# Running both halves' w2 sums ahead of their wo sums, a new share of MLP pieces among the attention units, and final wo sums that end one at a time

## The chip, the cores and the metric

One Trainium2 chip, one core. The metric is device time in microseconds (us) of one execution; lower is better. Executions of one kernel differ by 1 to 3 us, so a difference of a few us is read from two sources here: the clock, over several rounds on the same chip, and the trace, in which the start of every instruction is recorded.

## The reference, cut to what matters

The output is `x + A(xn) + B(xn)` with `xn = layernorm(x)`, 2048 tokens, width 1024. A is attention in four segments of 512 tokens with 32 heads of 32, plus a memory carried from segment to segment, and an output projection `wo`. B is a token-mixing MLP, `w2(gelu(w1 h))` along the token axis with a hidden size of 3584.

```python
for s in range(4):                                   # segment
    logits = einsum('bhqd,bhkd->bhqk', qs, ks) * scale + mask
    a_dot  = einsum('bhqk,bhkd->bhqd', softmax(logits), vs)
    num, den = phi(qs) @ M, phi(qs) @ z + 1e-06      # memory of the segments before
    o = g * num / den + (1 - g) * a_dot
    M, z = M + phi(ks)^T vs, z + sum(phi(ks))
A = concat(o) @ wo
B = (gelu(h^T w1 + b1) @ w2 + b2)^T                  # h = layernorm(xn)
```

## The kernel before: the parts that matter

The program first runs layernorm and the hidden layer of the MLP (896 matmuls of 128x512), which needs no attention. Then come 32 attention units, eight per segment, each with four heads. Each unit has three exponentiations on ScalarE (ACT), of about 1.9, 1.5 and 1.5 us in the trace. So that TensorE (PE) need not wait for them, pieces of the second MLP layer and of the output projection are put in between. One piece is one 128x512 matmul. Matmuls write into PSUM banks, eight buffers numbered 0 to 7 in this program; a bank can be written anew only when another engine has read its last result. There are 16 output chunks of 128 tokens and each has two halves of 512 columns. A half is a sum of 28 w2 pieces; for the twelve chunks of segments 0 to 2 ("fused" chunks), 8 wo pieces are added in the same PSUM bank. The chunks of segment 3 (12 to 15) come first, without wo; their wo sums are made in a tail.

In the code below, `logits` multiplies q by k, `weigh` multiplies the exponentials by v, and `combine` divides and gates on VectorE. The output of `combine` is transposed into one block of `oT` per unit, which the wo pieces read. The "k phi" is phi(k), made on ScalarE and VectorE after each k projection.

```python
def main_emit(self, n):                    # emit the next n pieces
    ...
    j, c, half, fused = self.main[self.main_k]     # one half after the other: 28 w2, then 8 wo
    b = self.main_bank                             # banks 6 and 7 in turn
    ...                                            # matmuls
    if end == total:
        fw.op("dve", lambda e: e.scalar_tensor_tensor(dst, self.bank(b), self.b2c[:, c:c + 1], dst, ...))  # bias add
        ...
        self.main_bank = 13 - b

def attention_and_out(self):
    ...
    for c in range(4):
        self.proj_v(0, c, c)
    for u in range(self.LEAD):             # LEAD = 2
        self.proj_q(u, 4 + u); self.proj_k(u, 6 + u)
        ...
    for u in range(N_UNIT):
        n0, n1, n2 = (9, 7, 6) if s == 0 else (10, 8, 8)      # n3: 6 or 10; 28 or 36 in all
        self.logits(u, 0)                  # 32-row matmuls into banks 0-3, then exp on ACT
        if u: self.combine(u - 1)          # VectorE
        self.main_emit(n0)
        self.logits(u, 1); self.main_emit(n1)
        self.logits(u, 2)
        ...                                # DMA transposes of k and of the combined output
        self.main_emit(n2)
        self.weigh(u, 0); self.weigh(u, 1)
        if un < N_UNIT: self.proj_q(un, 0)           # un = u + 2, bank 0
        self.weigh(u, 2)
        if m < 2 * N_SEG: self.proj_v(m, u % 4, 2)
        self.weigh(u, 3)
        if un < N_UNIT: self.proj_k(un, 1)           # bank 1
        self.main_emit(n3)
    self.main_emit(10 ** 6)
    self.tail()

def tail(self):
    self.combine(u)                        # unit 31
    ...                                    # load chunks 12-15 back: fin[0..3]
    for (i, h), b in zip(order, banks):    # eight sums of seven products ...
        if b == 3: self.o_transpose(u, 3)  # PE transpose and ACT copy ahead of the last
        ...
    for (i, h), b in zip(order, banks):    # ... then the eighth product of each
        ...
        fw.op("dve", ... tensor_tensor(dst, self.bank(b), dst, op=ALU.add))
        if h == 1: fw.dma(self.out_d[:, 4 * s + i, :], fin[i][:], ...)
```

The softmax here doesn't subtract the row's maximum and nothing guards it: scores larger than these inputs give would overflow.

## Time and profile before

| | before |
|---|---|
| time, median of the runs beside the changed kernel | 721.57 us (720.23 to 722.08) |
| span of the profiled execution | 720.2 us |
| PE busy | 97% |
| VectorE (DVE), ACT busy | 37%, 38% |
| from the last hidden-layer matmul to the end | 509.20 us |

Three lines of the page: its heading, the busy time of each engine with its share of the span and the number of instructions, and the shares of the chain of waits that ended last.

```profile
span 720.2 us, 11218 instructions
PE 701.0 (97%) x4818; PEld 324.6 (45%) x4818; DVE 263.1 (37%) x577; ACT 276.7 (38%) x314; POOL 111.1 (15%) x151
...
PE 93%; DVE 3%; ACT 2%; DMA 1%; issue 1%; SPq 0%; POOL 0%; DVEq 0%; ACTq 0%
```

PE bounds the kernel. How full it is can't be read from the 97%: a 128x512 matmul is recorded as 379 ns, but in the trace two of them start 215.5 ns apart, so the recorded end lies some 160 ns after the next one's start and hides short gaps. The Trainium skill says the same of this busy time (Perfetto Trace Analysis, "Identifying the Most-Contended Engine": it is not a good measure of how close a kernel is to its limit, because matmuls are pipelined), and its TensorE: Matmul & The Clock Gate, "Wait — 56ns, not 53.3ns?", gives 215.7 ns from start to start at 512 columns. So in what follows a wait is the time from one start to the next, less 0.2155 us per 512 columns, and less the 0.10 us that a change into or out of the 32-row logits costs in every unit.

Who waited for whom on PE (engine, line, what released it, us in total, times, longest; L192 is the helper that issues every matmul, so it tells the tile and not the place):

```profile
PE ps_all L192 <- POOL h L651: 3.5, 2, 2.7
PE ps_all L192 <- DVE h L647: 3.5, 1, 3.5
PE ps_all L192 <- ACT etmp_1584 L749: 2.2, 8, 0.3
PE ps_all L192 <- DVE warm L508: 1.3, 1, 1.3
PE ps_all L192 <- ACT pT L786: 1.0, 1, 1.0
PE ps_all L192 <- ACT xnT_69 L884: 0.7, 1, 0.7
PE ps_all L198 <- DMA brow_51<-in_B_b_dram: 0.4, 1, 0.4
PE ps_all L192 <- DVE ost_1579 L826: 0.4, 1, 0.4
PE ps_all L192 <- DVE ost_1580 L826: 0.4, 1, 0.4
```

Lines 1, 2, 4 and 7 belong to the start of the program, which the change does not touch. The others are the waits in the attention part and the tail that this list shows: eight of 0.3 us, one of 1.0, three of 0.4 to 0.7. Here is one of the eight, from the timeline around the start of unit 2 (start us, duration us, engine, line, operation, out<-in; in brackets the idle time before it and what ended it):

```profile
252.74 1.46 PE L192 MATMUL ps_all<-gT,w2h_912 128*128 128x512 bf16 x6
252.94 0.69 DVE L746 CAST kT_1570<-ps_all 128x512 bf16<-128x512 f32 x1 [0.90 <-PE ps_all L192]
253.73 0.60 ACT L749 ACTIVATE etmp_1584<-ps_all 128x512 bf16<-128x512 f32 x1 [2.55 <-DVE kT_1570 L746]
...
254.47 0.40 PE L192 MATMUL ps_all<-qT_1569,kT_1572 32*128 32x512 bf16 x4 [0.27 <-ACT etmp_1584 L749]
```

The k projection ends at 252.74 in bank 1. The bank is free when a cast (0.69) and an exponentiation (0.60) have read it, and only then may the next unit's logits write it, 1.73 us later. Six pieces take 6 x 0.2155 = 1.29 us. With the switch of 0.10, 0.33 us are lost. And the tail (the end of the ACT copy; the last two adds and stores):

```profile
709.82 0.39 PE L198 MATMUL ps_all<-ident,o_s_1582 128*128 128x128 bf16 x4
710.25 0.60 ACT L884 ACTIVATE xnT_69<-ps_all 128x512 bf16<-128x512 bf16 x1 [15.09 <-PE ps_all L198]
...
710.90 0.39 PE L192 MATMUL ps_all<-wo_sb,xnT_69 128*128 128x512 bf16 x1 [0.69 <-ACT xnT_69 L884]
...
716.44 1.27 DVE L1016 TENSOR_TENSOR fin_7771<-ps_all,fin_7771 128x512 bf16<-128x512 f32 x2
716.54 0.33 SPq L214 DMA_DIRECT2D out_dram<-fin_7770  x1
717.74 0.33 SPq L214 DMA_DIRECT2D out_dram<-fin_7771  x1
```

The last matmul starts at 713.93. All eight sums end within 1.5 us, so their eight adds queue on VectorE until 717.71, and the last store follows: 6.3 us from the last matmul's start to the end of the span.

### The profile page before, as it was taken

What the parts mean: (1) busy time and instruction counts of PE and PEld (TensorE: products, weight loads), DVE (VectorE), ACT (ScalarE), POOL (GpSimd) and SP (SyncE); (2) the same over time, 40 slices, a digit from 0 to 9 for tenths busy, and PEclk for the clock granted to TensorE, in tenths of its full rate; (3) what the DMA queues carried; (4) which work ended last, traced back from release to release, by engine and by line L of the source; (5) the groups of instructions that cost most, each with busy time, mean ns of one, the idle gap of its engine ahead of it and who ended that gap; (6) DMA issues with size and microseconds to landing.
All of it is one profiled execution on the core that took longest, in us unless ns stands there. A gap on an engine that the chain in (4) does not pass through costs nothing.

```text
span 720.2 us, 11218 instructions
## 1 busy us (share of the span) xinstructions
PE 701.0 (97%) x4818; PEld 324.6 (45%) x4818; DVE 263.1 (37%) x577; ACT 276.7 (38%) x314; POOL 111.1 (15%) x151
## 2 busy tenths in 40 slices
PE   6899999999999999999999999999999999999996
PEld 2344444444444444444444444444444444444442
DVE  4970000000002343344444545544555544344452
ACT  4551122111225445445444444443444444434420
POOL 1540000000001112211221111222111122111220
PEclk9999999999999999999999999999999999999999
DMA  9549677246016373872654625355352635527103
GB/s 269 142 115 177 144 190 192 64 112 124 12 60 163 66 125 87 127 118 63 123 117 87 126 44 126 75 109 120 79 125 45 126 86 97 111 53 117 30 27 114
DMA packets 211515, 77.17 MB, mean 107 GB/s; under 512 B 172554, under 2 KB 203274, under 8 KB 211466
## 3 DMA queue, kind: packets, MB, share of 16 engines
q1 hardware_dynamic: 211248, 76.43, 48.9%
q8 instruction: 38, 0.62, 0.4%
q14 instruction: 11, 0.09, 0.0%
q10 hardware_dynamic: 218, 0.02, 0.0%
HBM read 59.79 MB, written 5.24 MB: 90 GB/s over the span
## 4 chain that ended last, share of the span: by engine, by line
PE 93%; DVE 3%; ACT 2%; DMA 1%; issue 1%; SPq 0%; POOL 0%; DVEq 0%; ACTq 0%
PE ps_all L192 93%; DMA xin<-in_A_x_dram 1%; ACT etmp_1584 L749 1%; DVE kT_1570 L746 0%; DVE ln_st L606 0%; DVE kT_1572 L746 0%; DVE kT_1571 L746 0%; DVE ln_st L605 0%; ACT pT L786 0%; SPq L214 0%; DVE h L647 0%; ACT L749 0%; POOL h L651 0%; DVE fin_7771 L1016 0%; DVE fin_7770 L1016 0%
## 5 line engine op out<-in xcount | busy, mean ns | idle before, releaser
L786 ACT ACTIVATE pT<-ps_all 128x1536 bf16<-128x1536 f32 (+1 forms) x96 | 153.0, 1593 | 96.8 <-PE ps_all L192 96.8
L792 POOL TENSOR_SCALAR_AFFINE_SELECT pT<-pT 128x512 bf16<-128x512 bf16 x128 | 90.9, 723 | 561.5 <-ACT pT L786 561.5
L708 ACT ACTIVATE gT<-ps_all,b1c 128x512 bf16<-128x512 f32 x56 | 37.7, 689 | 134.5 <-PE ps_all L192 134.5
L192 PE MATMUL ps_all<-h,w1s_78 128*128 128x512 bf16 x320 | 73.9, 385 | 7.1 <-POOL h L651 3.5
L192 PE MATMUL ps_all<-h,w1s_79 128*128 128x512 bf16 x320 | 73.8, 385 | 0.0
L746 DVE CAST kT_1570<-ps_all 128x512 bf16<-128x512 f32 x11 | 7.6, 690 | 178.9 <-PE ps_all L192 178.9
L192 PE MATMUL ps_all<-gT,w2h_912 128*128 128x512 bf16 x224 | 56.3, 380 | 0.0
L192 PE MATMUL ps_all<-gT,w2h_914 128*128 128x512 bf16 x224 | 56.3, 380 | 0.0
L192 PE MATMUL ps_all<-h,w1s_80 128*128 128x512 bf16 x256 | 55.9, 379 | 0.0
L192 PE MATMUL ps_all<-gT,w2h_913 128*128 128x512 bf16 x224 | 53.9, 381 | 0.0
L192 PE MATMUL ps_all<-gT,w2h_911 128*128 128x512 bf16 x224 | 53.9, 381 | 0.0
L192 PEld LDWEIGHTS ps_all<-h,w1s_78 128*128 128x128 bf16 x320 | 31.4, 99 | 46.3 <-issue 8.5
L192 PEld LDWEIGHTS ps_all<-h,w1s_79 128*128 128x128 bf16 x320 | 31.7, 99 | 39.0 <-issue 2.3
L826 DVE CAST ost_1579<-ps_all 128x264 bf16<-128x264 f32 (+1 forms) x64 | 23.8, 394 | 69.2 <-PE ps_all L192 69.0
L826 DVE CAST ost_1580<-ps_all 128x264 bf16<-128x264 f32 (+1 forms) x64 | 23.8, 394 | 69.0 <-PE ps_all L192 68.9
L192 PEld LDWEIGHTS ps_all<-h,w1s_80 128*128 128x128 bf16 x256 | 25.0, 98 | 30.2
L749 ACT ACTIVATE etmp_1584<-ps_all 128x512 bf16<-128x512 f32 x24 | 14.3, 597 | 58.1 <-DVE kT_1572 L746 20.7
L192 PEld LDWEIGHTS ps_all<-gT,w2h_912 128*128 128x128 bf16 x224 | 20.6, 98 | 25.2 <-issue 2.5
L192 PEld LDWEIGHTS ps_all<-gT,w2h_914 128*128 128x128 bf16 x224 | 20.5, 98 | 24.7 <-issue 2.5
L192 PEld LDWEIGHTS ps_all<-gT,w2h_911 128*128 128x128 bf16 x224 | 19.3, 98 | 25.3 <-issue 6.4
L192 PEld LDWEIGHTS ps_all<-gT,w2h_913 128*128 128x128 bf16 x224 | 19.3, 98 | 25.3 <-issue 6.4
L192 PE MATMUL ps_all<-wo_sb,oT_1587 128*128 128x512 bf16 x128 | 30.2, 379 | 0.0
(154 smaller groups left out, 815.3 us busy)
## 6 DMA issues: line engine op xcount, KB each, us to landing
w1s_80<-in_B_w_dram SPq DMA_DIRECT2D x4, 1024.0 KB, 5.9
w1s_78<-in_B_w_dram SPq DMA_DIRECT2D x4, 1024.0 KB, 5.6
w1s_79<-in_B_w_dram SPq DMA_DIRECT2D x4, 1024.0 KB, 5.7
wq_907<-in_A_wq_dram SPq DMA_DIRECT2D x16, 256.0 KB, 3.5
wq_908<-in_A_wq_dram SPq DMA_DIRECT2D x16, 256.0 KB, 3.6
wk_909<-in_A_wk_dram SPq DMA_DIRECT2D x16, 256.0 KB, 3.8
wk_910<-in_A_wk_dram SPq DMA_DIRECT2D x16, 256.0 KB, 4.0
w2h_911<-in_B_w_dram SPq DMA_DIRECT2D x8, 448.0 KB, 4.8
```

The costliest lines, as they stand in the source:

```text
L192: ins = self.nc.tensor.matmul(*args, **kwargs)
L708: fw.op("act", lambda e: e.activation(self.gT[:, fc, half * 512:(half + 1) * 512], self.bank(b), ACT.Gelu_apprx_tanh, bias=self.b1c[:, fc: ...
L746: fw.op("dve", lambda e: e.tensor_copy(self.kT[k][:], self.bank(b)), reads=[self.R_bank[b]], writes=[self.R_kT[k]])
L749: fw.op("act", lambda e: e.activation(self.etmp[1][:], self.bank(b), ACT.Exp), reads=[self.R_bank[b]], writes=[self.R_etmp[1]])
L786: fw.op("act", lambda e: e.activation(self.pT[:, :, off:off + total], self.ps[:, 0:4, 0:total], ACT.Exp, scale=SCALE), reads=self.R_bank[0:4],
L792: fw.op("pool", lambda e: e.affine_select(d, d, pattern=[[0, 4], [1, P]], compare_op=ALU.is_ge, fill=0.0, base=0, channel_multiplier=-1), ...
L826: fw.op("dve", lambda e: e.tensor_copy(dst, self.ps[:, b, 0:n * VW]), reads=[self.R_bank[b]], writes=[self.R_ost[o][qb]])
```

## The change

Its intent: keep PE from waiting, with the same 4818 matmuls. (1) Within a fused chunk the w2 sums of both halves come first (bank 6 and bank 7), then the two wo sums. The first wo piece of a chunk is then 56 pieces after its start, not 28, so a chunk may begin earlier, before its segment's attention is finished. (2) That allows more pieces in the first segment: 32 per unit, 8 before unit 0, 34 per unit later, and pieces in place of the q projection that units 30 and 31 lack. (3) At the start q0 and k0 are projected ahead of v. (4) The final sums end one at a time and each half row is stored by itself. (5) `combine` is moved: behind the first pieces of the next unit, and for the last unit of a segment to that unit's own end, so that its block is there sooner.

```diff
     def main_init(self):
-        for n, c in enumerate(self.mlp_order):
-            for half in range(2):
-                self.main.append((n, c, half, c < 12))
+        for j, c in enumerate(self.mlp_order):
+            self.main += [(j, c, half, a, a + 14) for half in range(2) for a in (0, 14)]
+            if c < 12:
+                self.main += [(j, c, half, N_FCH, N_FCH + N_GRP) for half in range(2)]
 ...
-            b = self.main_bank
+            b, s = 6 + half, c // 4
 ...
     def attention_and_out(self):
+        self.proj_q(0, 4)
+        self.proj_k(0, 5)
+        self.k_transpose(0)
         for c in range(4):
             self.proj_v(0, c, c)
-        for u in range(self.LEAD):
-            self.proj_q(u, 4 + u)
-            self.proj_k(u, 6 + u)
-            if u == 0:
-                self.k_transpose(0)
+        self.proj_q(1, 4)
+        self.proj_k(1, 5)
+        self.main_emit(8)
 ...
             self.logits(u, 0)
-            if u:
-                self.combine(u - 1)
+            if u and last_of_seg(u - 1):
+                self.o_transpose_dma(u - 1)
             self.main_emit(n0)
+            if u and not last_of_seg(u - 1):
+                self.combine(u - 1)
 ...
             if un < N_UNIT:
                 self.proj_q(un, 0)
+            else:
+                self.main_emit(8)
 ...
+            if last_of_seg(u):
+                self.combine(u)
             self.main_emit(n3)
 ...
+    def share(u):
+        if u < N_UNIT - 4:
+            return (10, 8, 7, 7) if u < N_GRP else (10, 8, 8, 8)
+        return (10, 9, 8, 10) if u < N_UNIT - 2 else (10, 9, 8, 4)
 
     def tail(self):
-        order = [(i, h) for i in range(4) for h in range(2)]       # and two loops over all eight sums
 ...
+        def product(n, j0, j1):                                    # matmuls j0..j1-1 of sum n
 ...
+            fw.dma(self.out_d[:, 4 * s + i, h * 512:(h + 1) * 512], dst, reads=[R_fin[i][h]],
+                   writes=[self.R_out[4 * s + i]], is_output=True)
+
+        product(0, 0, 7)
+        product(1, 0, 7)
+        self.o_transpose(u, 6)
+        product(2, 0, 7)
+        for n in range(3):
+            product(n, 7, 8)
+        for n in range(3, 8):
+            product(n, 0, 8)
```

More of the change, by code (lines that the diff above doesn't have):

```diff
@@ L889, in main_init @@
         self.main = []
-        for n, c in enumerate(self.mlp_order):
-            for half in range(2):
-                self.main.append((n, c, half, c < 12))
+        for j, c in enumerate(self.mlp_order):
+            self.main += [(j, c, half, a, a + 14) for half in range(2) for a in (0, 14)]
+            if c < 12:
+                self.main += [(j, c, half, N_FCH, N_FCH + N_GRP) for half in range(2)]
         self.main_k = 0
         self.main_at = 0
-        self.main_bank = 6
     def main_emit(self, n):
@@ L899, in main_emit @@
         while n > 0 and self.main_k < len(self.main):
-            j, c, half, fused = self.main[self.main_k]
-            b = self.main_bank
-            at = self.main_at
-            total = N_FCH + (N_GRP if fused else 0)
-            if at == 0 and half == 0:
-                self.stg_ring.ensure(j)
-            s = c // 4
-            if at < N_FCH:
-                w, R_w = self.w2_ring.get(2 * j + at // 14)
-                end = min(at + n, (at // 14 + 1) * 14)
-                reads = [R_w] + [self.R_gT[fc][half] for fc in range(at, end)]
-            else:
-                end = min(at + n, total)
-                reads = [self.R_wo] + [self.R_oT[s % 2][jc - N_FCH] for jc in range(at, end)]
+            j, c, half, a, stop = self.main[self.main_k]
@@ new lines, in main_emit @@
+            a += self.main_at
+            end = min(a + n, stop)
+            total = N_FCH + (N_GRP if c < 12 else 0)
+            b, s = 6 + half, c // 4
+            if a == 0 and half == 0:
+                self.stg_ring.ensure(j)
+            if a < N_FCH:
+                w, R_w = self.w2_ring.get(2 * j + a // 14)
+                reads = [R_w] + [self.R_gT[fc][half] for fc in range(a, end)]
+            else:
+                reads = [self.R_wo] + [self.R_oT[s % 2][x - N_FCH] for x in range(a, end)]
@@ L914, in main_emit @@
             with fw.group(reads=reads, writes=[self.R_bank[b]]):
-                for x in range(at, end):
-                    st, sp = x == 0, x == total - 1
+                for x in range(a, end):
                     if x < N_FCH:
-                        fw.mm(self.bank(b), w[:, x % 14, :], self.gT[:, x, half * 512:(half + 1) * 512],
-                              start=st, stop=sp)
-                    else:
-                        jc = x - N_FCH
-                        fw.mm(self.bank(b), self.oT[s % 2][:, jc, (c % 4) * P:(c % 4 + 1) * P],
-                              self.wo_sb[:, jc, half * 512:(half + 1) * 512], start=st, stop=sp)
@@ L924, in main_emit @@
-            n -= end - at
-            self.main_at = end
+                        lhs, rhs = w[:, x % 14, :], self.gT[:, x, half * 512:(half + 1) * 512]
+                    else:
+                        lhs = self.oT[s % 2][:, x - N_FCH, (c % 4) * P:(c % 4 + 1) * P]
+                        rhs = self.wo_sb[:, x - N_FCH, half * 512:(half + 1) * 512]
+                    fw.mm(self.bank(b), lhs, rhs, start=(x == 0), stop=(x == total - 1))
+            n -= end - a
+            self.main_at += end - a
@@ L926, in main_emit @@
+            if end == stop:
+                self.main_k += 1
+                self.main_at = 0
             if end == total:
-                k = j % 3
-                dst = self.stg[k][:, half * 512:(half + 1) * 512]
+                stg, R_stg = self.stg[j % 3], self.R_stg[j % 3]
+                dst = stg[:, half * 512:(half + 1) * 512]
                 fw.op("dve", lambda e: e.scalar_tensor_tensor(dst, self.bank(b), self.b2c[:, c:c + 1], dst,
                                                               op0=ALU.add, op1=ALU.add),
-                      reads=[self.R_bank[b], self.R_b2c, self.R_stg[k]], writes=[self.R_stg[k]])
+                      reads=[self.R_bank[b], self.R_b2c, R_stg], writes=[R_stg])
@@ L932, in main_emit @@
                 if half == 1:
-                    fw.dma(self.out_d[:, c, :], self.stg[k][:], reads=[self.R_stg[k]], writes=[self.R_out[c]],
-                           is_output=True)
-                self.main_bank = 13 - b
-                self.main_at = 0
-                self.main_k += 1
+                    fw.dma(self.out_d[:, c, :], stg[:], reads=[R_stg], writes=[self.R_out[c]], is_output=True)
     def attention_and_out(self):
@@ L944, in attention_and_out, with last_of_seg @@
         self.stg_ring.ensure(0)
+        self.proj_q(0, 4)
+        self.proj_k(0, 5)
+        self.k_transpose(0)
         for c in range(4):
             self.proj_v(0, c, c)
-        for u in range(self.LEAD):
-            self.proj_q(u, 4 + u)
-            self.proj_k(u, 6 + u)
-            if u == 0:
-                self.k_transpose(0)
+        self.proj_q(1, 4)
+        self.proj_k(1, 5)
+        self.main_emit(8)
+        def last_of_seg(u):
+            return u % N_GRP == N_GRP - 1
         for u in range(N_UNIT):
             s = u // N_GRP
-            n = 28 if s == 0 else 36
-            n0, n1, n2 = (9, 7, 6) if s == 0 else (10, 8, 8)
-            n3 = n - n0 - n1 - n2
-            if u == 2 * N_GRP - N_GRP + 0:
+            un, m = u + self.LEAD, u // 4 + 1
+            n0, n1, n2, n3 = self.share(u)
+            if u == N_GRP:
                 wait = _after(*[self.R_xnT[c] for c in range(4)])
@@ L962, in attention_and_out @@
             self.logits(u, 0)
-            if u:
+            if u and last_of_seg(u - 1):
+                self.o_transpose_dma(u - 1)
+            self.main_emit(n0)
+            if u and not last_of_seg(u - 1):
                 self.combine(u - 1)
-            self.main_emit(n0)
             self.logits(u, 1)
@@ L970, in attention_and_out @@
                 self.k_transpose(u + 1)
-            if u:
+            if u and not last_of_seg(u - 1):
                 self.o_transpose_dma(u - 1)
@@ L975, in attention_and_out @@
             self.weigh(u, 1)
-            un = u + self.LEAD
             if un < N_UNIT:
                 self.proj_q(un, 0)
+            else:
+                self.main_emit(8)
             self.weigh(u, 2)
-            m = u // 4 + 1
             if m < 2 * N_SEG:
@@ L985, in attention_and_out @@
                 self.proj_k(un, 1)
+            if last_of_seg(u):
+                self.combine(u)
             self.main_emit(n3)
-        self.main_emit(10 ** 6)
+        assert self.main_k == len(self.main)
         self.tail()
+    @staticmethod
+    def share(u):
+        if u < N_UNIT - 4:
+            return (10, 8, 7, 7) if u < N_GRP else (10, 8, 8, 8)
+        return (10, 9, 8, 10) if u < N_UNIT - 2 else (10, 9, 8, 4)
     def tail(self):
         fw = self.fw
-        s = N_SEG - 1
+        s, u = N_SEG - 1, N_UNIT - 1
         e = _Arena(self.nc, self.early_base, self.early_end)
@@ L996, in tail @@
         R_fin = [[Res(f"fin{i}_{h}", wait) for h in range(2)] for i in range(4)]
-        u = N_UNIT - 1
-        self.combine(u)
         for i in range(4):
@@ L1001, in tail @@
                    record_reads=False)
-        order = [(i, h) for i in range(4) for h in range(2)]
-        banks = [6, 7, 0, 1, 2, 4, 5, 3]
-        for (i, h), b in zip(order, banks):
-            if b == 3:
-                self.o_transpose(u, 3)
-            with fw.group(reads=[self.R_wo] + self.R_oT[s % 2][0:7], writes=[self.R_bank[b]]):
-                for jc in range(7):
-                    fw.mm(self.bank(b), self.oT[s % 2][:, jc, i * P:(i + 1) * P],
-                          self.wo_sb[:, jc, h * 512:(h + 1) * 512], start=(jc == 0), stop=False)
-        for (i, h), b in zip(order, banks):
-            with fw.group(reads=[self.R_wo, self.R_oT[s % 2][7]], writes=[self.R_bank[b]]):
-                fw.mm(self.bank(b), self.oT[s % 2][:, 7, i * P:(i + 1) * P],
-                      self.wo_sb[:, 7, h * 512:(h + 1) * 512], start=False, stop=True)
+        def product(n, j0, j1):
+            i, h, b = n // 2, n % 2, (0, 1, 2, 3, 4, 5, 7, 6)[n]
+            with fw.group(reads=[self.R_wo] + self.R_oT[s % 2][j0:j1], writes=[self.R_bank[b]]):
+                for jc in range(j0, j1):
+                    fw.mm(self.bank(b), self.oT[s % 2][:, jc, i * P:(i + 1) * P],
+                          self.wo_sb[:, jc, h * 512:(h + 1) * 512], start=(jc == 0), stop=(jc == N_GRP - 1))
+            if j1 < N_GRP:
+                return
             dst = fin[i][:, h * 512:(h + 1) * 512]
@@ L1017, in tail @@
                   reads=[self.R_bank[b], R_fin[i][h]], writes=[R_fin[i][h]])
-            if h == 1:
-                fw.dma(self.out_d[:, 4 * s + i, :], fin[i][:], reads=R_fin[i], writes=[self.R_out[4 * s + i]],
-                       is_output=True)
+            fw.dma(self.out_d[:, 4 * s + i, h * 512:(h + 1) * 512], dst, reads=[R_fin[i][h]],
[8 more added lines that the diff above has]
+            product(n, 0, 8)
 _INS = ['A_x', 'A_wq', 'A_wk', 'A_wv', 'A_wo', 'A_beta', 'B_x', 'B_w1', 'B_b1', 'B_w2', 'B_b2']
```

## The prediction

> **What bounds the kernel now.** TensorE: the chain of waits puts 93% of the 720.2 us on PE matmuls, 3% on VectorE. Busy time overstates it: a 128x512 matmul is recorded as 379 ns, while two follow each other every 0.2155 us (timeline, start to start). The Trainium skill has the same (TensorE: Matmul & The Clock Gate, "Wait — 56ns, not 53.3ns?": 215.7 ns), so I count starts. After 30 us nearly every matmul starts when its predecessor has streamed. About 0.11 us is lost at each change into the 32-row logits; the skill's TensorEngine Tiling (Array Packing), "Key Properties", says that changing tiling mode drains the array. That stays.
>
> Waits left over, from start times:
> - unit 0: the second logits wait 1.1 us for the first exponentiation, delayed by copies and an activation of 1.28 us that come together;
> - the next eight units' first logits wait 0.32 us beyond the switch (chain: PE, cast 0.70, exp 0.61, PE): six pieces (1.29 us) don't cover the 1.73 us from the end of the k projection until bank 1 is free;
> - units 30 and 31, which have no projections: 0.46 us each, a weigh waiting for its bank's cast;
> - tail: 0.69 us for the ScalarE copy of the transposed block, then 6.3 us from the last matmul's start, since all eight sums end together: eight VectorE adds at 0.61 us, then a store that takes 2.5 us from the last add to the span's end.
>
> **What the change does.** Matmuls, bytes and ScalarE work stay; only waits can go.
> - Start: q0/k0 first, eight MLP pieces before unit 0: -1.1.
> - Seven pieces at the end of a first-segment unit: 1.51 us of cover; 8 x 0.215 = -1.7.
> - Pieces in place of the missing q projection: -0.9.
> - Transpose: the copy is covered by the third product (-0.7), but the last combine (2.5 us after the casts, a bias add before it) has just two products (3.0 us) ahead of the transpose: +0.5. Net -0.2.
> - One add (0.68 us) and a half-size store after the last matmul: 6.3 becomes 3.5: -2.8.
> - New: a fused chunk's bank 6 is needed again 8 pieces after its wo sum ends. At the end of a unit the bias add (0.75) stands behind the k phi (ends 2.64 us after the last k projection matmul), done at 3.36. By the piece order only chunk 1 to 2 (unit 10 to 11) needs the bank earlier, at 2.6: +0.8. Unit 8 first reads the last oT block 6.7 us after unit 7's k projection; combine, issue and DMA transpose (2.4 to 3.5 us from issue) need 6.3 to 7.4: +0.2.
>
> Sum: -5.7 us.
>
> **Prediction.** 715.6 us, eight times in ten between 713.0 and 718.2. Faster by over 2%: 0.02; within 2%: 0.97; slower by over 2%: 0.01.
>
> **What would show it.** Unit period in segment 0 about 14.76 us (14.11, plus four pieces, less 0.21); segments 1 and 2 about 15.19 (15.62 less two pieces); no 1.1 us gap in unit 0; 3.5 us from the last matmul's start to the end; one gap of 0.5 to 0.9 us early in unit 11, before chunk 2's first piece.
>
> **What would make it wrong.** More bank stalls than one, because bias adds queue behind combine on VectorE; oT transposes landing late behind weight loads; a late last combine; half-row stores that land no sooner than full ones.

## The result, and the profile after

The changed kernel took 714.76 us (median of four runs, 714.27 to 715.41) against 721.57 us before: 6.8 us less. The ratio is 0.9909, with a 95% interval of 0.9892 to 0.9926. A ratio here is the mean time of one kernel's fast runs over that of the other's of the same rounds, so it is not quite the ratio of the medians. That is within 2%, and the interval is well clear of 1.

```profile
span 712.6 us, 11149 instructions
PE 693.8 (97%) x4728; PEld 323.6 (45%) x4818; DVE 263.0 (37%) x577; ACT 276.9 (39%) x314; POOL 105.4 (15%) x151
...
PE 94%; DVE 2%; issue 1%; DMA 1%; ACT 0%; SPq 0%; POOL 0%; ACTq 0%
```

PE shows 4728 matmuls in place of 4818, but the weight loads are still 4818: no work has gone, 90 records are missing from this trace, one in about fifty. Each hole looks like a gap of exactly one piece. Such holes make up most of the line "issue" below; they are not waits.

```profile
PE ps_all L192 <- DVE h L647: 4.4, 1, 4.4
PE ps_all L192 <- POOL h L651: 2.6, 2, 2.2
PE ps_all L192 <- issue: 2.0, 12, 0.2
PE ps_all L192 <- DVE warm L508: 1.3, 1, 1.3
PE ps_all L192 <- DVE stg_1591 L930: 0.7, 1, 0.7
PE ps_all L198 <- DVE o_s_1582 L868: 0.3, 1, 0.3
```

All the waits of the attention part of before are gone from this list, and two are new: one for a bias add (`stg`) and one for the last combine (`o_s`). The start of unit 2 now:

```profile
254.07 1.24 PE L192 MATMUL ps_all<-gT,w2h_913 128*128 128x512 bf16 x5
254.27 0.69 DVE L746 CAST kT_1570<-ps_all 128x512 bf16<-128x512 f32 x1 [0.90 <-PE ps_all L192]
...
255.05 0.60 ACT L749 ACTIVATE etmp_1584<-ps_all 128x512 bf16<-128x512 f32 x1 [2.55 <-DVE kT_1570 L746]
255.15 0.59 PE L192 MATMUL ps_all<-gT,w2h_914 128*128 128x512 bf16 x2
...
255.79 0.40 PE L192 MATMUL ps_all<-qT_1569,kT_1572 32*128 32x512 bf16 x4
```

From the end of the k projection (254.07) to the logits (255.79) it is still 1.72 us, but seven pieces now lie in between. About 0.12 us of the 0.33 is left, too short to show in the list. The new wait in unit 11, before chunk 2's first piece:

```profile
389.36 0.69 DVE L719 SCALAR_TENSOR_TENSOR mtmp_1586<-kT_1570,mtmp_1586 128x512 bf16<-128x512 bf16 x1
...
389.56 0.60 PE L192 MATMUL ps_all<-wo_sb,oT_1587 128*128 128x512 bf16 x2
...
389.97 1.61 DVE L930 SCALAR_TENSOR_TENSOR stg_1591<-ps_all,b2c,stg_1591 128x512 bf16<-128x512 f32 x2
...
390.86 0.38 PE L192 MATMUL ps_all<-gT,w2h_911 128*128 128x512 bf16 x1 [0.69 <-DVE stg_1591 L930]
```

Two bias adds stand together in the third line. The first must empty bank 6 before chunk 2 can begin in it, and it starts only when VectorE is done with the k phi (first line). The tail:

```profile
698.39 0.40 PE L198 MATMUL ps_all<-ident,o_s_1582 128*128 128x128 bf16 x4 [0.25 <-DVE o_s_1582 L868]
...
709.62 0.69 DVE L1021 TENSOR_TENSOR fin_7792<-ps_all,fin_7792 128x512 bf16<-128x512 f32 x1 [1.03 <-PE ps_all L192]
710.37 0.33 SPq L214 DMA_DIRECT2D out_dram<-fin_7792  x1
```

One add and one half-row store follow the last matmul (its start is 709.20): 3.36 us to the end of the span in place of 6.30.

**A steadier measure.** The part before attention differs from execution to execution. In the thirteen profiles in the fast state the last hidden-layer matmul starts between 208.89 and 211.97 us, a range of 3.1 us in work that no kernel here changes. After that point two executions of the same kernel agree to 0.01 us (501.92 and 501.91 us to the end, for the changed kernel; it is the only pair of traces of one kernel in the fast state). So besides the time by the clock each experiment gets "the rest": the span less the start of the last hidden matmul. Before: 720.23 - 211.03 = 509.20. After: 712.56 - 210.64 = 501.92. The change is worth 7.28 us; the 7.7 us between the two spans holds 0.4 us of luck. Figures of the rest below are good to about 0.01 us.

### The profile page after: what moved, and what is told of

It reads as the page before. It is cut to its first block, busy times and chain, and to the rows that moved or that the text cites. A ratio compares the mean times of both kernels' runs of the same rounds, so it can differ in the third digit from the quotient of the medians.

```text
span 712.6 us, 11149 instructions
## 1 busy us (share of the span) xinstructions
PE 693.8 (97%) x4728; PEld 323.6 (45%) x4818; DVE 263.0 (37%) x577; ACT 276.9 (39%) x314; POOL 105.4 (15%) x151
## 4 chain that ended last, share of the span: by engine, by line
PE 94%; DVE 2%; issue 1%; DMA 1%; ACT 0%; SPq 0%; POOL 0%; ACTq 0%
PE ps_all L192 94%; DMA xin<-in_A_x_dram 1%; DVE ln_st L606 0%; DVE ln_st L605 0%; SPq L214 0%; DVE h L647 0%; DVE prod L864 0%; POOL h L651 0%; ACT junk L615 0%; ACT ln_rs L635 0%; DVE stg_1591 L930 0%; DVE stg_1589 L930 0%; DVE kT_1570 L746 0%; DVE ln_rs L634 0%; DVE fin_7792 L1021 0%
## 5 line engine op out<-in xcount | busy, mean ns | idle before, releaser
L792 POOL TENSOR_SCALAR_AFFINE_SELECT pT<-pT 128x512 bf16<-128x512 bf16 x128 | 84.9, 676 | 565.0 <-ACT pT L786 565.0
L192 PE MATMUL ps_all<-gT,w2h_913 128*128 128x512 bf16 x219 | 55.2, 380 | 0.4 <-issue 0.2
L192 PE MATMUL ps_all<-gT,w2h_911 128*128 128x512 bf16 x220 | 53.9, 380 | 1.0 <-DVE stg_1591 L930 0.7
L192 PE MATMUL ps_all<-gT,w2h_912 128*128 128x512 bf16 x215 | 53.6, 380 | 1.0 <-issue 0.8
L192 PE MATMUL ps_all<-gT,w2h_914 128*128 128x512 bf16 x217 | 53.9, 380 | 0.6 <-issue 0.3
```

What stands on the lines that cost most here:

```text
L192: ins = self.nc.tensor.matmul(*args, **kwargs)
L792: fw.op("pool", lambda e: e.affine_select(d, d, pattern=[[0, 4], [1, P]], compare_op=ALU.is_ge, fill=0.0, base=0, channel_multiplier=-1), ...
```

## The experiments

The theory from the prediction: PE's work is fixed, the time is that work plus a few waits, and they add up. Rivals: the gain comes from one part (the reorder itself, or the tail, or the mere number of pieces per unit), and waits that go are partly given back elsewhere. "Before" was timed beside each. All results were correct.

| run | median us | ratio to before (95%) | the rest, us |
|---|---|---|---|
| before | 720.32 to 721.57 | 1 | 509.20 |
| the change | 714.76 | 0.9909 (0.9892 to 0.9926) | 501.92 |
| r_after (the change again) | 713.07 | 0.9894 (0.9878 to 0.9909) | 501.91 |
| tail_only | 718.59 | 0.9959 (0.9946 to 0.9972) | 505.85 |
| reorder_only | 726.96 | 1.0078 (1.0066 to 1.0091) | 515.14 |
| first_only | 712.63 | 0.9879 (0.9865 to 0.9892) | 501.05 |
| seg0_front | 715.70 | 0.9931 (0.9918 to 0.9945) | 504.46 |
| old_start_8 | 713.28 | 0.9903 (0.9887 to 0.9920) | 501.90 |
| new_start_0 | 713.80 | 0.9910 (0.9895 to 0.9924) | 502.61 |
| no_qslot | 716.60 | 0.9937 (0.9921 to 0.9954) | 503.56 |
| no_qslot_own | 715.01 (the five fast runs alone 714.28) | 0.9905 (0.9888 to 0.9923) | not used |
| no_qslot_own_again | 714.08 | 0.9900 (0.9883 to 0.9918) | 502.49 |
| three_first | 712.86 | 0.9882 (0.9864 to 0.9901) | 500.60 |
| all_four | 712.86 | 0.9882 (0.9866 to 0.9898) | 499.66 |

The "slow state" is that of one execution, whose trace shows a granted TensorE clock of 0.655 where all the others have 0.99. Several expectations missed by the clock: r_after, first_only, seg0_front and old_start_8 came 1 to 2 us below their marks, which were reckoned from the change's first 714.76 us, and no_qslot and all_four came about 1 us above theirs. In the rest most came within 0.1 us of what was expected; reorder_only lost 0.3 us more, and no_qslot 0.7.

### r_after: the change once more

> The change itself again, for its spread beside the three others. Expected 714.8 us (713.8 to 715.8), and in its trace the same single stall of 0.85 us in unit 11 and unit periods of 14.65 and 15.19 us, to 0.02 us. If the stall was an accident of one execution, it is absent or elsewhere.

Measured: 713.07 us, below the expected range. The wait in unit 11 is 0.852 us (0.854 the first time), the unit periods are 14.65 and 15.19 us. The stall comes back in the same place, so it was not an accident of one execution.

### tail_only: the kernel before with the new tail alone

```diff
-        for (i, h), b in zip(order, banks):   # both loops
+        product(0, 0, 7)                      # as in the change, after self.combine(u)
+        ...
```

> The kernel before with only the new tail. Theory (the waits add up, and the tail is worth about half of the whole): 3.2 us from the last matmul's start to the end in place of 6.3, the wait around the transpose 0.4 in place of 0.7, so 3.3 us faster than before, about 718.2 us; unit periods as before (14.11, 15.62). Rival (the gain lies in the new share of the pieces, and the tail's adds were hidden behind the stores): under 1 us faster, 720.5 or more.

Measured: 718.59 us, the rest 3.35 us shorter than before. The last matmul's start to the end took 3.35 us, and the wait at the transpose 0.43 in place of 0.85 from start to start: 2.94 + 0.42 = 3.36. The unit periods are those of before. The theory holds, and the tail is a little under half of the change's 7.28 us.

### reorder_only: the kernel before with the new order of sums alone

```diff
-                self.main.append((n, c, half, c < 12))
+            self.main += [(j, c, half, a, a + 14) for half in range(2) for a in (0, 14)]
+            if c < 12:
+                self.main += [(j, c, half, N_FCH, N_FCH + N_GRP) for half in range(2)]
```

> The kernel before with only the new order of sums (both halves' w2 sums first, banks 6 and 7 fixed), its old share. Theory (the order only makes the new share possible and by itself costs bank waits): a chunk then takes exactly two units and ends at the end of one, so the next chunk's first piece waits for the bias add standing behind the k phi: about 0.8 us at the start of units 10, 12, 14, 16, 18, 20 and 22 (seven waits; none after that, as the last segment has no k phi), 5.6 us slower than before, about 727 us. Rival (the reorder itself is a gain, keeping wo sums away from late oT blocks): same or faster than before, 721.5 or less.

Measured: 726.96 us, 0.8% slower than before, the rest 5.93 us longer. The first line of the list of PE's waits and one of the seven places:

```profile
PE ps_all L192 <- DVE stg L930: 5.6, 7, 0.8
```

```profile
370.60 1.61 DVE L930 SCALAR_TENSOR_TENSOR stg<-ps_all,b2c,stg 128x512 bf16<-128x512 f32 x2
...
371.49 0.38 PE L192 MATMUL ps_all<-gT,w2h 128*128 128x512 bf16 x1 [0.80 <-DVE stg L930]
```

Seven waits at the starts of units 10, 12, 14, 16, 18, 20 and 22, as expected. From start to start each is 0.86 us, and the two-unit period grows by 0.85: 7 x 0.85 = 5.95. The reorder by itself is a loss. It pays only together with a share of pieces that puts nearly all chunk ends elsewhere, which the changed kernel's 34 pieces per unit do, with one exception.

### first_only: both halves ahead only where it is needed

```diff
-            self.main += [(j, c, half, a, a + 14) for half in range(2) for a in (0, 14)]
-            if c < 12:
-                self.main += [(j, c, half, N_FCH, N_FCH + N_GRP) for half in range(2)]
+            w2 = [[(j, c, half, a, a + 14) for a in (0, 14)] for half in range(2)]
+            wo = [[(j, c, half, N_FCH, N_FCH + N_GRP)] if c < 12 else [] for half in range(2)]
+            self.main += w2[0] + w2[1] + wo[0] + wo[1] if c % 4 == 0 else w2[0] + wo[0] + w2[1] + wo[1]
```

> The change, but both halves' w2 sums run ahead only in the first chunk of each segment (0, 4, 8); the other chunks as before, one half after the other, so that a bank comes back after 36 pieces, not 8. Theory (the wait in unit 11 is the bank, given back late): the 0.85 us gap is gone and nothing else moves, 0.85 us faster than the change, about 714.0. Rival (the gap is the weights of chunk 2 or the x tile arriving late): the gap stays in unit 11 and the time is that of the change.

Measured: 712.63 us, the rest 501.05, so 0.87 us less than the change. No wait for a bias add is left on PE, and unit 11's period is 15.19 us like its neighbours'. The wait was the bank. Only the first chunk of a segment meets blocks that are not there yet; the others gain nothing from having both halves ahead.

### seg0_front: the same number of pieces, in other places

```diff
-            return (10, 8, 7, 7) if u < N_GRP else (10, 8, 8, 8)
+            return (12, 8, 6, 6) if u < N_GRP else (10, 8, 8, 8)
```

> The change with the same 32 pieces in each first-segment unit, but placed 12, 8, 6, 6 in place of 10, 8, 7, 7. Theory (what counts is that seven pieces lie between the k projection and the next unit, and seven between the last logits and the q projection): the waits of before come back, 0.22 us more before each of units 1 to 8 and about 0.10 more before each q projection, period 14.97 in place of 14.65, 8 x 0.32 = 2.5 us slower than the change, about 717.3. Rival (it is the number of pieces in a unit that covers ScalarE): period stays 14.65, time that of the change.

Measured: 715.70 us, the rest 2.54 us longer than the change's; period 14.97 us. Before the logits 0.33 us are lost again and before the q projection 0.10. The number of pieces in a unit does not cover ScalarE; the number between one use of a bank and the next does. The 0.10 us is a wait that the prediction had overlooked: the q projection writes bank 0, which the unit's last exponentiation (1.45 us) still reads when only six pieces lie between them.

### old_start_8 and new_start_0: the order or the eight pieces

```diff
 # old_start_8
-        self.proj_q(0, 4); self.proj_k(0, 5); self.k_transpose(0)
         for c in range(4):
             self.proj_v(0, c, c)
-        self.proj_q(1, 4); self.proj_k(1, 5)
+        self.proj_q(0, 4); self.proj_k(0, 6); self.k_transpose(0)
+        self.proj_q(1, 5); self.proj_k(1, 7)
         self.main_emit(8)
 # new_start_0: the change without
-        self.main_emit(8)
```

> The change with the old order at the start (v, then q0, k0, q1, k1 in banks 4, 6, 5, 7) but with its eight pieces before unit 0. If the eight pieces are what removed the 1.1 us wait of unit 0: no such wait, time that of the change within 0.3 us. If it was the order (q0 and k0 ahead of v): the 1.1 us wait is back, about 715.9.

> The change with its new order at the start but without the eight pieces before unit 0 (they are done at the end, where the share has eight to spare). If the eight pieces are what counts: unit 0's second logits wait 0.7 to 1.0 us again. If the order is: no wait there. All later pieces come eight earlier in the order, so other bank waits may appear and are read from the trace; the verdict is the gap in unit 0, not the time.

Measured: with the old order and eight pieces there is no wait in unit 0 and the rest is 501.90 us, that of the change. With the new order and no pieces unit 0 waits 0.71 us. So the eight pieces remove the wait; beside them the order adds nothing, and without them it helps only in part (0.71 in place of 1.10; of these 0.39 us, 0.22 are the time of one piece, since ten pieces in place of nine lie ahead of the second logits). The total of new_start_0 is 0.70 us longer than the change's although two other waits went (0.85 and 0.41); the next run shows why.

### no_qslot, no_qslot_own and its repetition: pieces for the missing q projection

```diff
 # no_qslot
             if un < N_UNIT:
                 self.proj_q(un, 0)
-            else:
-                self.main_emit(8)
 ...
-        return (10, 9, 8, 10) if u < N_UNIT - 2 else (10, 9, 8, 4)
+        return (10, 9, 8, 10) if u < N_UNIT - 2 else (10, 9, 8, 12)
```

> The change without the pieces in place of the missing q projection in units 30 and 31; they are done at the end of the unit. Theory: the wait of the third weigh for its bank's cast is back, 0.46 us in each of the two units, so 0.9 us slower than the change, about 715.7; the last combine then has pieces ahead of it and the transpose may wait less, up to 0.4 us of that given back. Rival (the slot is worth nothing): time that of the change.

Measured: 716.60 us, the rest 1.65 us longer than the change's. The two waits are back, 0.52 us each from start to start, and the transpose waits no more (0.41 less): 0.63 us. Another 1.05 us was not foreseen. The last store came late; the last add and the stores around it:

```profile
711.14 0.69 DVE L1019 TENSOR_TENSOR fin<-ps_all,fin 128x512 bf16<-128x512 f32 x1 [1.03 <-PE ps_all L192]
...
712.93 0.33 SPq L214 DMA_DIRECT2D out_dram<-fin  x1
```

The add ends at 711.83, the store is issued at 712.93. The records of landings show the store before it landing at 712.87. In the change's tail both half-row stores of a block claim the same output resource, so the second waits until the first has landed. All stores leave one queue in order, so the next pair waits behind them. That makes four pairs in a row, 2.2 to 2.7 us each, and the chain begins when the first add is done. With the first adds late, the last store is late. To test it, the claim was taken away; the two halves write different columns, and each store still waits for its own add.

```diff
 # no_qslot_own, and no_qslot_own_again
-            fw.dma(self.out_d[:, 4 * s + i, h * 512:(h + 1) * 512], dst, reads=[R_fin[i][h]],
-                   writes=[self.R_out[4 * s + i]], is_output=True)
+            fw.dma(self.out_d[:, 4 * s + i, h * 512:(h + 1) * 512], dst, reads=[R_fin[i][h]], is_output=True)
```

> The kernel without pieces in the q slot (it took 503.57 us from the last hidden matmul to the end, 1.67 more than the change, where 0.92 was expected), with one line undone: the two half-row stores of a block no longer both claim the same output resource. Theory (the second half's store waits until the first half's has landed, 1.8 to 2.2 us after its issue, so the four pairs form a chain that was late at the end): the last store is issued right after the last add, 1.05 us sooner, 502.5 us from the last hidden matmul to the end. Rival (half-row stores are simply slow to issue or to land when several are under way): 503.5 again, the last store issued a microsecond after the last add.

The profiled execution was slow (1019 us, granted clock 0.655), so its trace was not used.

> The kernel of no_qslot_own once more, unchanged, because its profile fell in the slow state (granted clock 0.655), where the matmuls between two stores take half as long again and hide the question. In the fast state: theory (the second half-row store waited for the first to land) 502.5 us from the last hidden matmul to the end, the last store issued within 0.05 us of the last add; rival (half-row stores are slow by themselves) 503.5, the last store a microsecond after the last add.

```profile
710.21 0.69 DVE L1019 TENSOR_TENSOR fin<-ps_all,fin 128x512 bf16<-128x512 f32 x1 [1.03 <-PE ps_all L192]
710.93 0.33 SPq L214 DMA_DIRECT2D out_dram<-fin  x1
```

Measured: the rest 502.49 us, 1.08 less than no_qslot. The add ends at 710.90 and the store is issued at 710.93. The rival falls. In the changed kernel the same chain is there and just not late: its last store was issued at 710.37, the store before it landed at 710.31 and the last add ended at 710.31. (The pairs before it did not hold it up: the first store of the last pair was issued at 708.61, just after its own add.) And in new_start_0 the span ends 4.62 us after the last matmul's start, in place of 3.36: the same cause, by the same signs (a last store at 710.01, after an add that ended at 708.69 and a store that landed at 709.95), though there it was not tested by itself.

### three_first and all_four: taking the rest away

```diff
 # three_first = first_only, and
-        product(0, 0, 7); product(1, 0, 7)
+        for n in range(3):
+            product(n, 0, 7)
         self.o_transpose(u, 6)
-        product(2, 0, 7)
-        for n in range(3):
+        product(3, 0, 7)
+        for n in range(4):
             product(n, 7, 8)
-        for n in range(3, 8):
+        for n in range(4, 8):
             product(n, 0, 8)
 # and the stores of no_qslot_own.   all_four = three_first, and
-            return (10, 8, 7, 7) if u < N_GRP else (10, 8, 8, 8)
+            return (10, 7, 7, 8) if u < N_GRP else (10, 8, 8, 8)
```

> The kernel with both halves ahead in chunks 0, 4 and 8 only, and three products (not two) before the transpose, a fourth to cover its ScalarE copy, and the stores of the halves free of each other. Expected: no wait before the transpose (0.41 us gone), no wait after it, last store right after the last add: 500.6 us from the last hidden matmul to the end, against 501.05 without this and 501.9 in the change. If the first adds, which come later, hold back the rest: 501.0 or more.

> The same with the first segment's 32 pieces placed 10, 7, 7, 8: the eighth at the end of the unit covers the 0.12 us left before each of units 1 to 8, and seven after the second logits were enough in the kernel before. Expected: unit period 14.53 in place of 14.65, 0.94 us less, 499.7 us from the last hidden matmul to the end; about 711.0 to 711.8 us by the clock, 1.3% faster than before. If seven pieces in the middle don't cover the exponentiation of the second logits: the wait moves there and the period stays at 14.65.

Measured: the rest is 500.60 us for three_first and 499.66 us for all_four, whose first-segment period is 14.53 us. Apart from the holes of missing records, no wait longer than 0.06 us is left on PE from unit 0 to the last matmul. What PE's list of waits shows for all_four:

```profile
PE ps_all L192 <- DVE h L647: 3.9, 1, 3.9
PE ps_all L192 <- POOL h L651: 3.6, 2, 2.7
PE ps_all L198 <- DMA brow<-in_B_b_dram: 2.0, 1, 2.0
PE ps_all L192 <- issue: 1.7, 11, 0.2
PE ps_all L192 <- DVE warm L508: 1.3, 1, 1.3
```

Only the start of the program and the holes. By the trace all_four is 2.25 us shorter than the change in the part after the hidden layer. By the clock it is 1.2% faster than before (0.9882); it took 712.86 us, where 711.0 to 711.8 were expected. Against the change (0.9909 and 0.9894) the intervals overlap, and it does not differ from three_first at all (712.86 both). The profiled executions show how that can be: in all_four's the last hidden matmul started at 211.97 us, in three_first's at 210.16.

## Why the prediction was right, point by point

The predicted time was 715.6 us (713.0 to 718.2), the measured one 714.76 (713.07 in r_after). The terms, against the waits from start to start in the two traces:

| term | predicted us | measured us | shown by |
|---|---|---|---|
| wait in unit 0 | -1.1 | -1.10 | trace; the eight pieces, old_start_8 and new_start_0 |
| first logits of units 1 to 8 | -1.7 | 8 x (0.333 - 0.117) = -1.73 | trace, seg0_front |
| q projection in units 0 to 7 | not seen | 8 x 0.103 = -0.82 | trace, seg0_front |
| units 30 and 31 | -0.9 | 2 x 0.52 = -1.04 | trace, no_qslot |
| transpose in the tail | -0.2 | 0.414 - 0.853 = -0.44 | trace, tail_only |
| after the last matmul | -2.8 | 3.36 - 6.30 = -2.94 | trace, tail_only |
| bank 6, chunk 1 to 2 | +0.8 | +0.85 | trace, first_only |
| last oT block in unit 8 | +0.2 | 0 | trace |
| sum | -5.7 | -7.22 (rest: -7.28) | |

**What held.** The main claim: matmuls stay, only waits can go, and they add up on PE. The place of the one new stall was found from the order of the pieces alone, and the run that should have had seven of them had seven, in the units named. The segment 1 and 2 period came out at 15.19 us as stated.

**What was off.** By the trace the sum was 1.6 us too small (5.7 for 7.28). The first difference by the clock, 6.8 us, hides part of that; the one of r_after, 8.1 us, does not. The largest slip is a term that was missing: the first-segment period was put at 14.76 us and came out at 14.65. The shortest wait on the prediction's list has 0.32 us; the wait of 0.10 us before each q projection is not on it and occurs eight times. Together these are worth about as much as the one bank stall. Second, the wait at the transpose was counted as 0.69 us, the idle time after the recorded end; from start to start it was 0.85. The same correction makes 0.46 us into 0.52 for units 30 and 31. Third, the last oT block: the DMA transpose landed by 348.19 us and PE reached it at 348.65, so its 0.2 us never came; it took 2.48 us from issue, near the lower end of the 2.4 to 3.5 us that were reckoned with. Fourth, "q0/k0 first" was listed with the eight pieces as the cure for unit 0; the order is worth nothing beside the pieces.

**What was right by luck.** The tail's term counted an add and a store. It did not see that the half-row stores wait for one another. In this kernel the first store of the last pair lands 1.70 us after its issue, and the adds come 1.73 us apart, so the last store is free just when the last add is done; in no_qslot the chain cost 1.05 us.

The start of the program is outside the argument: the two spans differ by 7.67 us, of which 0.39 come from an earlier end of the hidden layer in the second one.

## What to carry to other kernels

When one engine is full, a change that moves work around can win only the waits, so list every wait from start to start, short ones too, and multiply by how often each occurs: 0.10 us eight times weighs as much as one stall of 0.85. Filler works by its place, between a bank's last reader and its next writer, not by its amount; and an order of sums that gives a bank back late must be checked against where in the other engine's queue the read-out falls. When one store is split into two, check that the two don't claim the same resource in the program, or the second waits for the first to land, as here.

## What the Trainium skill lacked or had wrong

- TensorE: Matmul & The Clock Gate, "Back-to-back issue gap", gives about 131 ns per matmul as the sustained rate of weight load and matmul pairs at 512 columns and about 81 ns at 128. In every trace here in the fast state such pairs start 215.5 ns apart at 512 columns (over two thousand pairs in each, every matmul with its own weight load), and the four transposes of 128 columns in the tail of before 56 ns apart. The section's other formula, which it gives for an isolated matmul (512 columns over 2.4 GHz plus 2.5 ns), fits.
- TensorEngine Tiling (Array Packing), "Key Properties", says that changing the tiling mode drains the array, but not what that costs. Here a matmul of 32 rows starts 0.10 us later than a 128-row one would after the same predecessor (0.312 us from start to start in place of 0.2155), in every unit, whatever fills it. That the drain is what takes this time is not shown.
- DMA: Bandwidth & Descriptors, "Anatomy of one DMA", gives a fixed cost of about 2.0 us for a DMA, with a fit made on the GpSimd path, and no such fit for the sync engine's queue. In the changed kernel a half-row store of 128 KB from the sync engine's queue had landed 1.70 us after its issue (708.61 to 710.31); the four full-row stores of 256 KB in the tail of before took 2.0 us.
- Perfetto Trace Analysis does not say that matmul records can be missing: 4728 of 4818 in the changed kernel's trace, one in about fifty, each hole looking like a gap of one matmul. The count of weight loads (4818) shows it.
- No page consulted has the slow state of a program on one core: one execution of no_qslot_own took 1020.71 us at a granted clock of 0.655, the five others 713.30 to 715.94. What caused it stays open.
